# Fused attention and two MLPs on one core: q and k loaded as sixteen consecutive tokens per partition, with some events of a hand-made schedule moved

## The chip, the cores and the metric

The kernel runs on one core of one Trainium2 chip. The metric is the device time of one execution in microseconds (us); lower is better. In the rows, PE is the matrix engine (TensorE), DVE VectorE, ACT ScalarE, POOL GpSimd, and SP the engine whose queue issues the DMA transfers. L12 is line 12 of the kernel before.

## What is computed

Eight batches, eight heads, 576 tokens of 64 numbers each go through attention inside chunks of 64 tokens. The result, laid out as 4608 tokens of 512 numbers, goes through two MLPs, all in float32.

```python
    # attention: B, H, S, D = 8, 8, 576, 64; chunk = 64
    scores = scale * np.matmul(q_c, k_c.transpose(0, 1, 2, 4, 3))
    scores = scores - np.max(scores, axis=-1, keepdims=True)
    attn = np.exp(scores)
    attn = attn / (np.sum(attn, axis=-1, keepdims=True) + 1e-09)
    out = np.matmul(attn, v_c)
    ...
    # first MLP: 4608 x 512, 512 x 2048, 2048 x 512
    h = x @ w_in
    r = np.maximum(h, 0.0)
    g = r * r
    return (g @ w_out).astype(np.float32)
    ...
    # second MLP, same sizes
    h = x @ w_in
    h2 = h * h
    h3 = h2 * h
    P = a[0] + a[1] * h + a[2] * h2 + a[3] * h3
    Q = 1.0 + np.abs(b[0]) * np.abs(h) + np.abs(b[1]) * h2
    g = P / (Q + 1e-6)
    return (g @ w_out).astype(np.float32)
```

## The kernel before

**Float32 on PE.** A float32 product is made of three matmuls on the parts hi and lo of both operands (`mm3`, L463 to L467). So every matrix that PE reads is first split: a copy that rounds to hi (`copy`, L220 on ACT, L222 on DVE or POOL) and a subtraction that leaves lo (`split_lo`, L225).

**Two stages.** From 0 to about 560 us attention and the first MLP run interleaved; after that come planned units in which PE has hardly a pause. The first MLP goes over blocks of 512 tokens and 16 slices f of the hidden width. For the slice with number s, `mm_h(s)` makes 12 matmuls into one of two PSUM banks called h; `act1(s)` makes relu (L587) and its square (L588) on ACT, then hi gh and lo gl; `mm_out1(s)` makes 12 matmuls from gh and gl into four accumulators acc. So one s costs PE 24 matmuls, about 5.5 us. `mm_out1(s)` runs two s behind.

**Attention.** Tokens form 36 tiles of 128, treated in pairs. A pair with start t0 (13.55, 18.55, 22.55, 26.55 up to 58.55 by fours, then 62.3 and 66.3; the unit is one s) has these steps:

- at t0, `mm_pv2` (L730, L733) takes the pair before: 64 small matmuls of attention weights and v, into both h banks. They are emptied at t0 + 0.1, by `x2_hi` on ACT and `x2_lo` on DVE (hi and lo, kept in SBUF), or by `x1_raw`, one bank on ACT and one on DVE (sent to DRAM), and only then can the next `mm_h` write them;
- `mm_s` (L706) at t0 makes the scores of the pair's first tile from q and k, one s later those of the second; softmax follows (L775, L790, L795, L800, L807), and a transposition of its result by DVE (`s_tr`, L814) with copies between partitions on ACT (`s_mv`);
- q and k of a pair come in 8 loads (`load_qk`, four for q into the room qs, four for k into ks, some cut in two at a batch's end). In them 32 partitions hold tokens t*32 + r, so every token is a run of 256 bytes. `tr` (L661) turns blocks of 32x32 on DVE: q and k of the first tile and of the second; `tr_mv` copies on ACT what lies in the wrong partitions, and `tr_part` (L672) turns the rest, on 32 partitions at a time, into the places these copies left. A room can be loaded again once it is read. The very first pair has another layout.

**The first MLP's x** of some tiles is also prepared for the unit stage: DRAM to a buffer room (L433), four sums on POOL (L441), hi on ACT (`xq_hi`, L220, 128x7x128), lo on POOL (`xq_lo`, L225, two instructions), and a store (`xq_store`, L458).

**Order.** `manual_schedule` collects events with `at(t, fn, args)`, adds a number from the table `MOVED` if the event's name stands there, sorts by time and issues in that order. The position in that list is the position on every engine the event uses. `mm_out1(s)` stands at s + 2.5, but for the s just before a pair's t0 (s in `early`) at s + 1.551, which is a moment after t0: so PE has `mm_pv2`, `mm_s`, then this one `mm_out1`. For the pair at 26.55 this is the `mm_out1` of s = 25.

Of the kernel before, what the change touches and what calls it, by code (L numbers as in the profile page):

```python
# [99 lines left out]


@with_exitstack
def attn_moe_moe_kernel(
# [1648 lines left out]
```

## Time and profile before

| | us |
|---|---|
| median of 3 runs | 1651.41 (1650.15 to 1653.93) |
| the profiled execution | 1650.9 |
| its span | 1649.1 |
| PE busy in it | 1592.4 (97%) |
| DVE, ACT, POOL busy | 1053.2, 1097.6, 1070.5 |
| PE busy from 560 us on | 1083.36 of 1089.00 |
| granted PE clock, mean | 0.987 of full speed |

PE is the engine that sets the time; a microsecond leaves the total where PE stands idle or runs at a lower clock, and from 560 us on it has almost none of either. The 1.8 us between the profiled time and its span lie outside of the program's instructions.

### The profile page before, as it was taken

Reading aid. Unit: us, or ns where it says so; the run is one execution under the profiler, and the core shown is the slowest. Engines: PE = TensorE matmul, PEld = TensorE weight load, DVE = VectorE, ACT = ScalarE, POOL = GpSimd, SP = SyncE. Lnnn points to the kernel's source line nnn. Section 1 sums busy time; section 2 is a strip of 40 time slices with the busy share of each in tenths; the row PEclk is TensorE's granted clock in tenths of the full one; section 3 lists DMA queues with packets and bytes.
Section 4 is the critical chain, followed back from the end, with each engine's and each line's share of the span. In section 5 each row is a group of like instructions: output and inputs, shape, how many; then the busy total and the mean of one; then the engine's idle time right before and its main releaser. Section 6 shows DMA issues by size and latency. Waiting matters only on the chain.

```text
span 1649.1 us, 26183 instructions
## 1 busy us (share of the span) xinstructions
PE 1592.4 (97%) x9069; PEld 1308.0 (79%) x9069; DVE 1053.2 (64%) x1498; ACT 1097.6 (67%) x1796; POOL 1070.5 (65%) x1065
## 2 busy tenths in 40 slices
PE   8989999999788999999999999999999999999998
PEld 7867777878566888888878888888888888888887
DVE  6877877777552333233327788878877888788640
ACT  5855556667565556455557787888788878777651
POOL 3645264638662888487847885888588857565554
PEclk9989999999899999999999999999999999999999
DMA  9845788887899899988899999989998997666644
GB/s 248 238 110 147 202 246 252 252 241 224 253 276 370 281 296 301 357 276 284 289 386 326 318 302 370 299 268 300 364 304 269 299 364 256 202 208 203 198 148 146
DMA packets 380356, 440.08 MB, mean 267 GB/s; under 512 B 136896, under 2 KB 260032, under 8 KB 379200
## 3 DMA queue, kind: packets, MB, share of 16 engines
q1 hardware_dynamic: 380224, 438.40, 83.0%
q8 instruction: 73, 1.20, 0.3%
q14 instruction: 59, 0.48, 0.1%
HBM read 318.77 MB, written 119.54 MB: 266 GB/s over the span
## 4 chain that ended last, share of the span: by engine, by line
PE 71%; DMA 8%; ACT 5%; DVE 5%; SPq 4%; POOL 4%; issue 2%; DVEq 0%; ACTq 0%; POOLq 0%
PE acc L465 13%; PE acc L467 13%; PE acc L466 13%; PE h L465 11%; PE h L467 11%; PE h L466 11%; DMA w2q<-st 2%; SPq L638 2%; DMA w2o<-st 1%; ACT at L220 1%; DMA qs<-in_q_dram 1%; SPq L622 1%; DMA ks<-in_k_dram 1%; SPq L836 1%; DVE wc L267 1%
## 5 line engine op out<-in xcount | busy, mean ns | idle before, releaser
L225 POOL TENSOR_TENSOR gl<-spare,gh 128x512 fp32r<-128x512 f32 x200 | 269.1, 1348 | 103.5 <-ACT gh L220 95.0
L1128 POOL TENSOR_TENSOR t<-t,r 128x512 f32<-128x512 f32 x144 | 188.0, 1306 | 150.5 <-ACT t L1120 144.4
L465 PE MATMUL h<-x,w 128*128 128x512 f32 (+1 forms) x648 | 256.2, 395 | 8.4 <-ACT spare L580 6.5
L466 PE MATMUL h<-x,w 128*128 128x512 f32 (+1 forms) x648 | 252.7, 390 | 0.3 <-DVE x L225 0.3
L467 PE MATMUL h<-x,w 128*128 128x512 f32 (+1 forms) x648 | 252.4, 389 | 0.0
L465 PE MATMUL acc<-gh,w 128*128 128x512 f32 x576 | 230.3, 400 | 10.2 <-ACT ev L220 5.2
L466 PE MATMUL acc<-gl,w 128*128 128x512 f32 x576 | 227.5, 395 | 0.0
L467 PE MATMUL acc<-gh,w 128*128 128x512 f32 x576 | 227.5, 395 | 0.0
L466 PE MATMUL acc<-w,gh 128*128 128x512 f32 x575 | 223.8, 389 | 0.0
L467 PE MATMUL acc<-w,gh 128*128 128x512 f32 x575 | 223.8, 389 | 0.0
L465 PE MATMUL acc<-w,gl 128*128 128x512 f32 x575 | 223.8, 389 | 0.0
L465 PE MATMUL h<-w,w 128*128 128x512 f32 x416 | 162.1, 390 | 5.1 <-DVE h L1104 3.7
L467 PE MATMUL h<-w,w 128*128 128x512 f32 x416 | 162.2, 390 | 0.0
L466 PE MATMUL h<-w,w 128*128 128x512 f32 x416 | 162.1, 390 | 0.0
L225 DVE TENSOR_TENSOR w<-w 128x512 fp32r<-128x512 f32 x64 | 68.1, 1068 | 131.2 <-ACT w L220 130.1
L465 PEld LDWEIGHTS h<-x,w 128*128 128x128 f32 x648 | 122.8, 190 | 35.6 <-ACT spare L580 7.3
L467 PEld LDWEIGHTS h<-x,w 128*128 128x128 f32 x648 | 122.9, 190 | 25.4
L466 PEld LDWEIGHTS h<-x,w 128*128 128x128 f32 x648 | 123.0, 190 | 24.9 <-DVE x L225 0.5
L465 PEld LDWEIGHTS acc<-gh,w 128*128 128x128 f32 x576 | 110.0, 191 | 37.6 <-ACT ev L220 6.5
L467 PEld LDWEIGHTS acc<-gh,w 128*128 128x128 f32 x576 | 110.0, 191 | 23.4
L466 PEld LDWEIGHTS acc<-gl,w 128*128 128x128 f32 x576 | 110.2, 191 | 22.4
L467 PEld LDWEIGHTS acc<-w,gh 128*128 128x128 f32 x575 | 108.0, 188 | 22.4
(178 smaller groups left out, 3420.3 us busy)
## 6 DMA issues: line engine op xcount, KB each, us to landing
w<-w2o SPq DMA_DIRECT2D x144, 512.0 KB, 4.8
w<-w2q SPq DMA_DIRECT2D x256, 256.0 KB, 5.4
w<-w1q SPq DMA_DIRECT2D x112, 256.0 KB, 5.6
x2q<-xroom SPq DMA_DIRECT2D x32, 896.0 KB, 6.5
st<-in_moe_w_in_dram SPq DMA_DIRECT2D x32, 512.0 KB, 5.5
st<-in_moe_w_out_dram SPq DMA_DIRECT2D x32, 512.0 KB, 6.1
w2q<-st SPq DMA_DIRECT2D x32, 512.0 KB, 4.6
w<-w1r SPq DMA_DIRECT2D x64, 256.0 KB, 5.6
```

The lines of the kernel that those rows point to most:

```text
L220: nc.scalar.activation(out=o, in_=x, func=ACTF.Copy)
L225: eng.tensor_tensor(out=o, in0=x, in1=hi.bitcast(F32), op=ALU.subtract)
L267: nc.vector.scalar_tensor_tensor(out=c, in0=c, scalar=3, in1=st[:, :, 0], op0=ALU.logical_shift_left, op1=ALU.bitwise_or)
L465: nc.tensor.matmul(out=o, lhsT=al, rhs=bh, start=first and i == 0, stop=False, **kw)
L466: nc.tensor.matmul(out=o, lhsT=ah, rhs=bl, start=False, stop=False, **kw)
L467: nc.tensor.matmul(out=o, lhsT=ah, rhs=bh, start=False, stop=last and i == len(pairs) - 1, **kw)
L622: nc.sync.dma_start(out=x[off:off + n, c], in_=v[bb, h0:h0 + 4, ss:ss + n, :].rearrange("h p d -> p h d"))
L638: nc.sync.dma_start(out=x.rearrange("p (t e) d -> p t (e d)", e=2)[Q:Q + 32, off // 32:(off + n) // 32], in_=src[bb, 2 * i + hp, ss:ss + n ...
L836: nc.sync.dma_start(out=x[:, t], in_={"q": q, "k": k_in, "v": v}[nm][0, 4 * k:4 * k + 4, t0:t0 + 128, :].rearrange("h r d -> r h d"))
L1128: nc.gpsimd.tensor_tensor(out=t, in0=t, in1=T["r", b, f], op=ALU.mult)
```

## The change

**Loads.** For every pair but the first, a partition now takes 16 consecutive tokens in one run of 4 KB. The same bytes go to n/16 partitions instead of 32: the 8 loads of a pair have 8 x 512 packets of 256 B before and 8 x 32 of 4 KB after. Pieces of a load that is cut in two now go to, say, 8 and 24 partitions.

**Transpositions.** For the columns of a turned tile to be in token order again, `blocks()` gives DVE an output in which neighbouring elements of a block of 32 lie 16 elements (64 bytes) apart. What is read keeps its shape.

```diff
         if u:
             b, i = divmod(NAT + 2 * u, TPB)
-            Q = 32 * (2 * (hp % 2) + hp // 2)
             for off, n, bb, ss in runs(b * NB, NB):
-                nc.sync.dma_start(
-                    out=x.rearrange("p (t e) d -> p t (e d)", e=2)[Q:Q + 32, off // 32:(off + n) // 32],
-                    in_=src[bb, 2 * i + hp, ss:ss + n, :].rearrange("(t r) d -> r t d", r=32))
+                Q = 32 * (2 * (hp % 2) + hp // 2) + off // 16
+                nc.sync.dma_start(out=x[Q:Q + n // 16].rearrange("p a d -> p (a d)"),
+                                  in_=src[bb, 2 * i + hp, ss:ss + n, :].rearrange("(r t) d -> r (t d)", t=16))
             return
...
     def blocks(x):
-        return x.rearrange("p a (g r) -> p (a g) r", r=32)
+        return x.rearrange("p a j -> p (a j)").rearrange("p (r t) -> p t r", t=16)
```

On DVE the turned tiles around the pair at 26.55 stand in the same places. Before (q, k are the turned tiles, qs, ks the rooms, u and at the softmax's):

```order
L814 STREAM_TRANSPOSE at_2352<-e_2299 128x8x2x32
L661 STREAM_TRANSPOSE q_2371<-qs_626 128x512
L661 STREAM_TRANSPOSE k_2373<-ks_758 128x512
L661 STREAM_TRANSPOSE q_2378<-qs_626 128x512
L661 STREAM_TRANSPOSE k_2380<-ks_758 128x512
L267 SCALAR_TENSOR_TENSOR wc_2375<-wc_2375,st_2252 128x512
L222 CAST gh_2396<-r_2398 128x512
L225 TENSOR_TENSOR gl_2397<-r_2398,gh_2396 128x512
L672 STREAM_TRANSPOSE q_2378<-qs_626 32x512 x2
L672 STREAM_TRANSPOSE k_2380<-ks_758 32x512 x2
```

The same place on DVE after:

```order
L779 STREAM_TRANSPOSE at_2352<-e_2299 128x8x2x32
L626 STREAM_TRANSPOSE q_2371<-qs_626 128x16x32
L626 STREAM_TRANSPOSE k_2373<-ks_758 128x16x32
L626 STREAM_TRANSPOSE q_2378<-qs_626 128x16x32
L626 STREAM_TRANSPOSE k_2380<-ks_758 128x16x32
L233 SCALAR_TENSOR_TENSOR wc_2375<-wc_2375,st_2252 128x512
L188 CAST gh_2396<-r_2398 128x512
L191 TENSOR_TENSOR gl_2397<-r_2398,gh_2396 128x512
L637 STREAM_TRANSPOSE q_2378<-qs_626 32x16x32 x2
L637 STREAM_TRANSPOSE k_2380<-ks_758 32x16x32 x2
```

The order is the same; the eight transpositions of q and k (four of L661, four of L672, in 14 pairs) have the other output.

**The table.** Old entries keep their numbers but one (a weight's `w_join:(0,7,1)`). New are `mm_out1` of s = 8 to 59 at -0.1 (but 17 at +0.165 and 19 at -0.2), s = 4 at +0.35, and some 25 single events, of which a line:

```diff
 MOVED = {
...
+    'xq_hi:2': -1.0, 'mm_pv2:8,9': 0.05, 'mm_out1:17': 0.165, 'w1q_sum2:6': 0.1, 's_norm:17': -0.2,
...
```

On PE, the -0.1 carries the early `mm_out1` across t0 at 11 pairs (13.55 and 22.55 to 58.55). Before, at 26.55, where w_8_91 holds the slices of two `mm_out1` and h is the next `mm_h`:

```order
L465 MATMUL acc_596<-gh,w_8_91 128x512
L466 MATMUL acc_596<-gl,w_8_91 128x512
L467 MATMUL acc_596<-gh,w_8_91 128x512
L733 MATMUL h<-at,v 64x64 x32
L706 MATMUL a<-k,q 64x64 x16
L465 MATMUL acc_593<-gh,w_8_91 128x512
L466 MATMUL acc_593<-gl,w_8_91 128x512
L467 MATMUL acc_593<-gh,w_8_91 128x512
```

The same place on PE after, from the last three matmuls of the early `mm_out1`:

```order
L431 MATMUL acc_596<-gh,w_8_91 128x512
L432 MATMUL acc_596<-gl,w_8_91 128x512
L433 MATMUL acc_596<-gh,w_8_91 128x512
L698 MATMUL h<-at,v 64x64 x32
L671 MATMUL a<-k,q 64x64 x16
L431 MATMUL h<-x_68,w_10_83 128x512
L432 MATMUL h<-x_69,w_10_83 128x512
L433 MATMUL h<-x_68,w_10_83 128x512
```

The 12 matmuls of the early `mm_out1` now stand ahead of `mm_pv2` and `mm_s`, and the next `mm_h` right behind. At 18.55 it is `mm_s` alone that goes ahead of `mm_pv2`; at 62.3 and 66.3 nothing changes on PE.

On POOL one `xq_lo` goes ahead of four sums of weights (`w1q_sum2:6`, L324). Before, with room_4458 the room of `xq_hi(2)` and `xq_lo(2)`:

```order
L314 TENSOR_TENSOR wc<-w_12_85 128x512
L314 TENSOR_TENSOR wc<-w_13_86 128x512
L324 TENSOR_TENSOR ee<-wc 128x256
L324 TENSOR_TENSOR ee<-ee,wc 128x256
L324 TENSOR_TENSOR wc<-wc 128x2x128
L324 TENSOR_TENSOR wc<-wc,ee 128x2x128
L225 TENSOR_TENSOR room_4458<-room_4458 128x4x128
L225 TENSOR_TENSOR room_4458<-room_4458 128x3x128
L441 TENSOR_TENSOR room_4607<-room_4607 128x128 x4
```

After:

```order
L280 TENSOR_TENSOR wc<-w_12_85 128x512
L280 TENSOR_TENSOR wc<-w_13_86 128x512
L191 TENSOR_TENSOR room_4458<-room_4458 128x4x128
L191 TENSOR_TENSOR room_4458<-room_4458 128x3x128
L290 TENSOR_TENSOR ee<-wc 128x256
L290 TENSOR_TENSOR ee<-ee,wc 128x256
L290 TENSOR_TENSOR wc<-wc 128x2x128
L290 TENSOR_TENSOR wc<-wc,ee 128x2x128
L407 TENSOR_TENSOR room_4605<-room_4605 128x128 x4
```

The two instructions of `xq_lo(2)` moved ahead of four. On ACT `xq_hi(2)` moved too: it stood behind the copies of q and k of the pair at 58.55, right ahead of the relu of s = 58, and stands now ahead of the copies of at that come before all these. On SP a handful of loads swap with a neighbour. The stage after 560 us keeps its order.

## Rows read from the trace of the kernel before

**Rows 1.** The page: busy time by engine, granted clock, DMA packets.

```profile
PE 1592.4 (97%) x9069; PEld 1308.0 (79%) x9069; DVE 1053.2 (64%) x1498; ACT 1097.6 (67%) x1796; POOL 1070.5 (65%) x1065
...
DMA packets 380356, 440.08 MB, mean 267 GB/s; under 512 B 136896, under 2 KB 260032, under 8 KB 379200
```

**Rows 2.** Busy time by stretch; columns as in the first line.

```profile
core 0: us, PE busy (x) PEld busy (x) DVE busy (x) ACT busy (x) POOL busy (x), PEclk, DMA share, GB/s
...
320.00:400.00 80.00, 75.93 (x674) 60.97 (x673) 60.45 (x92) 51.90 (x95) 46.95 (x50) 0.98 0.84 240
...
440.00:480.00 40.00, 27.09 (x214) 21.88 (x215) 21.45 (x34) 23.43 (x41) 25.01 (x32) 0.79 0.87 250
...
560.00:1649.00 1089.00, 1083.36 (x4780) 896.58 (x4778) 669.17 (x908) 756.96 (x1188) 773.01 (x764) 1.00 0.85 282
```

**Rows 3.** PE's waits, 0 to 560 us: us in total, times, longest.

```profile
PE h L733 <- ACT spare L580: 10.4, 4, 8.9
PE h L733 <- ACT r L587: 9.6, 7, 2.5
...
PE acc L465 <- ACT ev L220: 5.2, 3, 2.8
```

**Rows 4.** PE in order of time: start, length, instruction, [idle before it, releaser].

```profile
198.84 0.33 PE L733 MATMUL h<-at,v 64*64 64x64 f32 x2
201.68 1.10 PE L733 MATMUL h<-at,v 64*64 64x64 f32 x59 [2.52 <-ACT r L587]
...
446.33 0.47 PE L733 MATMUL h<-at,v 64*64 64x64 f32 x2 [8.86 <-ACT spare L580]
```

**Rows 5.** ACT in order of time, three stretches.

```profile
118.55 1.09 ACT L220 ACTIVATE x<-h 128x512 fp32r<-128x512 f32 x2 [4.95 <-PE h L730]
...
201.03 0.60 ACT L587 ACTIVATE r<-h 128x512 f32<-128x512 f32 x1
...
445.68 0.60 ACT L580 ACTIVATE spare<-h 128x512 f32<-128x512 f32 x1
```

**Rows 6.** DVE in order of time, three stretches.

```profile
119.20 1.29 DVE L225 TENSOR_TENSOR x<-h,x 128x512 fp32r<-128x512 f32 x2
...
200.12 0.98 DVE L225 TENSOR_TENSOR gl<-r,gh 128x512 fp32r<-128x512 f32 x1
...
429.95 0.65 DVE L267 SCALAR_TENSOR_TENSOR wc<-wc,st 128x512 int32<-128x512 int32 x1
...
441.14 0.71 DVE L661 STREAM_TRANSPOSE q<-qs 128x512 f32<-128x512 f32 x1 [8.60 <-DMA qs<-in_q_dram]
```

**Rows 7.** SP, the issuing queue, in order of time, 412 to 440 us.

```profile
420.45 0.38 SPq L458 DMA_DIRECT2D x1q<-room  x1
...
435.97 1.58 SPq L638 DMA_DIRECT2D qs<-in_q_dram  x1
```

**Rows 8.** SP's waits, 412 to 440 us: us in total, times, longest.

```profile
SPq L458 <- POOL room L225: 3.5, 1, 3.5
```

**Rows 9.** POOL in order of time, 407 to 422 us.

```profile
414.83 0.73 POOL L324 TENSOR_TENSOR ee<-wc 128x256 f32<-128x256 f32 x1
...
418.17 2.25 POOL L225 TENSOR_TENSOR room<-room 128x512 fp32r<-128x512 f32 x2
```

**Rows 10.** Busy time by stretch around the longest pause, columns as in rows 2.

```profile
442.00:452.30 10.30, 5.30 (x101) 4.61 (x102) 7.56 (x11) 5.87 (x10) 6.94 (x10) 0.50 0.79 251
```

**Rows 11.** DVE by line and shape, 80 to 520 us: busy, mean ns | idle before.

```profile
L267 DVE SCALAR_TENSOR_TENSOR wc<-wc,st 128x512 int32<-128x512 int32 x28 | 24.0, 864 | 7.3 <-ACT st L261 6.9
...
L672 DVE STREAM_TRANSPOSE q<-qs 32x512 f32<-32x512 f32 x28 | 19.7, 703 | 2.4 <-ACT q L220 1.6
...
L661 DVE STREAM_TRANSPOSE q<-qs 128x512 f32<-128x512 f32 x28 | 18.9, 674 | 10.0 <-DMA qs<-in_q_dram 10.0
L814 DVE STREAM_TRANSPOSE at<-e 128x512 f32<-128x512 f32 x28 | 18.7, 669 | 0.0
```

**Rows 12.** The page's costliest groups: DVE's dearest 512-column instruction.

```profile
L225 DVE TENSOR_TENSOR w<-w 128x512 fp32r<-128x512 f32 x64 | 68.1, 1068 | 131.2 <-ACT w L220 130.1
```

More of the change, by code (lines that the diff above doesn't have):

```diff
@@ L64 @@
     "xh2": 'V', "xh4": 'V'}
-MOVED = {
[34 rows of a table removed]
+MOVED = {'w_words:(0,3,0)': -14.15, 'w_words:(0,0,1)': -13.45, 'w_words:(0,2,0)': -11.949, 'w_load:0,4,0': -11.348, 'w_join:(0,2,0)': -11.648, 'w_load:0,2,1': -11.348, 'w_join:(0,3,0)': -11.847, 'w_load:0,5,0': -10.747, 'w_join:(0,0,1)': -12.246, 'w_load:0,4,1': -13.245, 'w_load:0,6,0': -0.499, 'w_words:(0,1,1)': -0.527, 'w_split:(0,3,0)': -0.202, 'w_join:(0,1,1)': -0.8, 'first:half110': 11.902, 'w_words:(0,4,0)': -0.401, 'act1:1': 0.401, 'load_tok:4,v,v0': 1.799, 'load_qk:0,qs,1': 0.899, 'load_qk:0,qs,2': 0.301, 'w_words:(0,2,1)': -0.236, 'w_split:(0,1,1)': 0.465, 's_exp:4': 0.015, 'w_load:0,5,1': -0.02, 'act1:2': -0.084, 'w_words:(0,5,0)': 0.517, 'w_join:(0,5,0)': 0.201, 'w_join:(0,2,1)': -0.022, 'w_split:(0,5,0)': 0.079, 'a_ps:5': -2.202, 'tr_second:5': 0.597, 'f_tr:4': 0.597, 'f_copy:4,0,0': -0.152, 'w_load:0,7,1': -0.802, 'load_qk:0,qs,3': 1.2, 'f_copy:4,0,1': -0.15, 'w_words:(0,6,0)': 0.149, 'w_words:(0,7,0)': -0.324, 'tr_copy:5,q': 0.602, 'w_split:(0,3,1)': -0.047, 'f_copy:4,1,1': 0.153, 'w_load:0,6,1': 0.068, 'tr_copy:5,k': 0.821, 'load_tok:5,v,v1': 0.497, 'w_join:(0,6,0)': 0.902, 'mm_s:5,5': -0.199, 'w_words:(0,4,1)': 0.597, 'w_join:(0,7,0)': 0.698, 'w_load:0,9,1': -1.239, 'w_split:(0,6,0)': 0.862, 'w_words:(0,5,1)': 0.299, 'w_split:(0,7,0)': 0.501, 'w_load:0,10,0': 0.448, 'w_join:(0,5,1)': -0.001, 's_exp:5': 0.048, 'w_join:(0,4,1)': 0.699, 'w_words:(0,8,0)': 0.1, 'act1:5': 0.001, 'load_qk:0,ks,3': 0.899, 'w_split:(0,4,1)': 0.399, 'w_words:(0,7,1)': -1.2, 'w_join:(0,7,1)': -1.165, 'w_load:0,11,0': 0.662, 'act1:6': -0.154, 'w_load:0,8,1': 1, 'f_tr:5': 0.599, 'w_words:(0,6,1)': 0.551, 'w_load:0,13,0': -0.299, 'w_join:(0,6,1)': 0.201, 'w_load:0,12,0': 0.205, 'w_split:(0,6,1)': -0.048, 'w_load:0,10,1': -1.647, 'w_split:(0,7,1)': -0.546, 'f_copy:5,1,0': 0.549, 'w_words:(0,10,0)': 0.101, 'w_join:(0,10,0)': 0.196, 'tr:6,ks,k': 1.648, 'f_copy:5,1,1': 1.049, 'act1:8': 0.001, 'load_tok:6,v,v0': 1.459, 'w_words:(0,9,1)': -0.39, 'w_split:(0,10,0)': 0.35, 'mm_s:6,6': 0.001, 'tr:7,ks,k': 1.202, 'w_join:(0,8,1)': 0.335, 'mm_s:7,6': 0.6, 'w_split:(0,8,1)': -0.05, 'x2_lo:1,5': 0.752, 'w_join:(0,9,1)': 0.143, 'act1:9': 0.5, 'w_split:(0,12,0)': -0.199, 'w_words:(0,13,0)': 0.102, 'f_copy:6,0,0': -0.45, 'w_load:0,15,0': 0.051, 'w_join:(0,13,0)': -0.249, 'w_words:(0,10,1)': -0.322, 'w_join:(0,10,1)': -0.401, 's_exp:7': -0.05, 'w_split:(0,9,1)': 0.55, 's_norm:7': -0.073, 'w_load:0,11,1': -0.022, 'f_copy:6,1,0': 0.079, 'f_copy:6,1,1': 0.08, 'act1:10': 0.081, 'w_split:(0,13,0)': 0.3, 'w_load:0,12,1': -0.199, 'w_split:(0,10,1)': 0.101, 'f_copy:7,0,0': -0.551, 'w_load:0,13,1': -0.293, 'w_join:(0,15,0)': -0.047, 'w_split:(0,14,0)': 0.349, 'w_load:0,15,1': -1.142, 'f_copy:7,0,1': 0.301, 'f_copy:7,1,0': 0.443, 'f_copy:7,1,1': 0.444, 'w_join:(0,12,1)': -0.248, 'w_words:(0,13,1)': 0.101, 'w_join:(0,13,1)': -0.149, 'w_split:(0,13,1)': 0.601, 'w_words:(0,14,1)': 0.998, 'w_join:(0,14,1)': 0.751, 'w_join:(0,15,1)': 0.252, 'w_split:(0,14,1)': 0.999, 'w_split:(0,15,1)': 0.898, 's_tr:8': 0.85, 's_mv:8': 0.85, 's_tr:9': 1.06, 's_mv:9': 1.06, 'act1:17': 0.799, 'x1_store:34,35': -0.1, 'mm_pv2:8,9': 0.05, 'mm_h:32': 0.05, 'xq_lo:0': 0.6, 'o_lo:1': -0.1, 'mm_out1:4': 0.35, 'load_qk:1,ks,3': -0.2, 'mm_out1:8': -0.1, 'mm_out1:9': -0.1, 'mm_out1:10': -0.1, 'mm_out1:11': -0.1, 'mm_out1:12': -0.1, 'mm_out1:13': -0.1, 'mm_out1:14': -0.1, 'mm_out1:15': -0.1, 'mm_out1:16': -0.1, 'mm_out1:17': 0.165, 'mm_out1:18': -0.1, 'mm_out1:19': -0.2, 'mm_out1:20': -0.1, 'mm_out1:21': -0.1, 'mm_out1:22': -0.1, 'mm_out1:23': -0.1, 'mm_out1:24': -0.1, 'mm_out1:25': -0.1, 'mm_out1:26': -0.1, 'mm_out1:27': -0.1, 'mm_out1:28': -0.1, 'mm_out1:29': -0.1, 'mm_out1:30': -0.1, 'mm_out1:31': -0.1, 'mm_out1:32': -0.1, 'mm_out1:33': -0.1, 'mm_out1:34': -0.1, 'mm_out1:35': -0.1, 'mm_out1:36': -0.1, 'mm_out1:37': -0.1, 'mm_out1:38': -0.1, 'mm_out1:39': -0.1, 'mm_out1:40': -0.1, 'mm_out1:41': -0.1, 'mm_out1:42': -0.1, 'mm_out1:43': -0.1, 'mm_out1:44': -0.1, 'mm_out1:45': -0.1, 'mm_out1:46': -0.1, 'mm_out1:47': -0.1, 'mm_out1:48': -0.1, 'mm_out1:49': -0.1, 'mm_out1:50': -0.1, 'mm_out1:51': -0.1, 'mm_out1:52': -0.1, 'mm_out1:53': -0.1, 'mm_out1:54': -0.1, 'mm_out1:55': -0.1, 'mm_out1:56': -0.1, 'mm_out1:57': -0.1, 'mm_out1:58': -0.1, 'mm_out1:59': -0.1, 'evac1:0,2': -0.1, 'w1q_store:2,0': 0.2, 'xq_hi:2': -1.0, 's_norm:17': -0.2, 'op_hi:4': -0.35, 'load_v:18': 0.2, 'act1:67': 1.0, 's_exp:35': -0.2, 'w1q_sum2:0': 0.1, 'w1q_sum2:1': 0.1, 'w1q_sum2:2': 0.1, 'w1q_sum2:3': 0.1, 'w1q_sum2:4': 0.05, 'w1q_sum2:5': 0.1, 'w1q_sum2:6': 0.1, 'w1q_sum2:7': 0.1, 'load_qk:14,qs,2': 0.2, 'xp_load:2,0': -1.0, 'o_hi:3': -0.35, 'i_load:6': 1.0}
```

34 rows, old and new, of the table MOVED are left out of this document.

## The prediction

> **What bounds the kernel now.** I read the page first [rows 1]: PE is busy 97% of the span, so what is to be had is PE's idle time, some 57 us, and its time at a low clock. The table by stretches [rows 2] shows where: from 560 us on PE is busy 1083.36 of 1089 us at clock 1.00, and nothing of this change is in there. In 320 to 400 us PE is busy 75.93 of 80; in 440 to 480 only 27.09 of 40, at 0.79 of the clock. So the change is worth what it does to PE's pauses before 560 us. Next PE's waits [rows 3]: the largest are those of `mm_pv2` (L733) for the h banks, which relu on ACT must first read: 9.6 us in 7 waits for L587, the longest 2.5, and 10.4 for L580 in 4, of which one pause of 8.9. Waits for the emptying of acc by ACT come to 5.2. Last I went along the engines in order of time at two of these places.
>
> At 199 us [rows 4] PE has begun `mm_pv2` at 198.84, and idles 2.52 us for the relu of s0 = 26, which ACT makes at 201.03, 0.60 long [rows 5]. Meanwhile PE could do another thing: the early `mm_out1`, whose last input gl DVE ends at 200.12 + 0.98 = 201.10 [rows 6].
>
> At 437 us PE idles 8.86, until 446.33 [rows 4]. It waits for the relu at 445.68 [rows 5]; ACT comes to that only behind the copies of q and k, and these wait for DVE, which had been idle 8.60 us and began q's transposition at 441.14, when qs landed [rows 6]. That load was issued at 435.97 and took 1.58 to issue [rows 7]. SP's queue goes strictly in order, and in it stands, earlier, the store x1q at 420.45, which had waited 3.5 us for POOL [rows 7, 8]. POOL, before the lo that this store needs (418.17), did the four sums L324 from 414.83 on [rows 9]. So one chain runs from four small sums on POOL to the longest pause of the kernel.
>
> **The change part by part.**
>
> *The store at 420 us.* `xq_lo(2)` goes ahead of the four sums: it starts 418.17 - 414.83 = 3.34 us sooner, and `xq_hi(2)`, which it needs, was moved up on ACT as well. The store's wait of 3.5 falls to about 0.2, and everything behind it in the queue can come up to 3.34 us sooner: five loads of v, the next room's load, loads and stores of weights, the loads of q and k. The four sums end 2.25 us later than before (the lo's length [rows 9]); they feed a store of weights for the unit stage, long before these are read, so I put nothing down. The issue of the late qs took 1.58 us where the store took 0.38 [rows 7]; with 32 packets in place of 512 it may cost that much too, 1.2 less. Sum 3.34 + 1.2 = 4.5 us off the pause of 8.86. Ends: 0, if something else in the queue holds it as long, and 8.9, the whole pause.
>
> *The clock behind it.* In 442.00 to 452.30 the granted clock is 0.50, PE is busy 5.30 us there [rows 10]: at full clock these are 2.65. A pause of some 4.4 us in place of 8.86 leaves part of it; I take -2, ends 0 and -2.65.
>
> *The early output block.* At 11 pairs the 12 matmuls now stand before `mm_pv2`. What they cover is the wait for relu (L587), 9.6 us in all [rows 3]. What is new: `mm_h` follows `mm_pv2` and `mm_s` at once, and must wait until the h bank is emptied. There are two kinds of pair. Where x stays in SBUF (13.55, 22.55, 34.55, 38.55, 50.55, 54.55), the first bank is free when ACT's hi (118.55) and the first of DVE's two lo are done, at 119.20 + 1.29/2 = 119.85 [rows 5, 6]; `mm_s` is over some 0.9 us sooner. So 0.9 us becomes visible that twelve matmuls covered. Where x goes to DRAM (26.55, 30.55, 42.55, 46.55, 58.55) one copy frees each bank, and about 0.1 is seen. At 26.55 the early block itself waits for gl until 201.10, 2.26 us after 198.84 in place of 2.52: a gain of 0.2 at most. I went through the 11 pairs and 18.55 in this way: four gain 0.65 to 1.7 (18.55, 30.55, 46.55, 58.55, sum -4.65), five lose 0.35 to 0.95 (13.55, 22.55, 34.55, 50.55, 54.55, sum +4.0), three stay within 0.2 (-0.3). Sum -1. Ends: -9.6, if all of these waits go, and 11 x 0.9 = +10, if none does. I stay near the middle, since gl is made by DVE straight after the relu before it, so that the two things PE can wait for are about equally late.
>
> *The transpositions.* 112 of them (8 in each of 14 pairs) now write at a step of 64 bytes. Before they take 0.674 to 0.703 us, whether 128 partitions or 32 [rows 11]. No row shows DVE writing at a step from element to element. Nearest: L814 writes its blocks of 32 words to scattered places for 0.669; L267 reads every second word of one source, in the mean 0.864, yet 0.65 where nothing disturbs it [rows 6, 11]; the dearest 512-column instruction takes 1.068 [rows 12]. So the price is between 0 and about +0.4 each (1.068 - 0.669); a gain can't be excluded, but the element count is the same. I take 0, since L267 undisturbed shows that a step on the read side alone costs nothing, and carry +0.4 as a rival.
>
> The Trainium skill speaks against this part: "Vector Engine (DVE) Microarchitecture Reference", section 5.2 "Measured stream behaviour on trn2", gives 1.054 ns per column when all is contiguous, 1.71 when the destination hops on every element, and 2.50 when it steps by 24 words, full rate needing pairs of adjacent words. By it a transposition of 512 columns would cost an estimated +0.34 to +0.74 us. L267's 0.65 with a source that has no adjacent pairs [rows 6] doesn't agree with that rule for reads of every second word; for writes no row here decides.
>
> *The loads themselves.* 14 pairs x 8 x 512 = 57,344 packets of 256 B become 3,584 of 4 KB, out of 380,356 [rows 1]. The 16 DMA engines are busy 0.84 to 0.87 of the time in this stage [rows 2], so transfers behind these loads land sooner. But PE seldom waits for one: DVE's 10.0 us of waits for qs are nearly all the 8.60 at 441 [rows 6, 11]. I put -1 for this and the remaining single moves together; ends 0 and -5, about what the waits for acc come to [rows 3].
>
> The sum: 1650.9 (the profiled time) - 4.5 - 2 - 1 - 1 = 1642.4. The median lies 0.5 above the profiled run, so 1643.
>
> **The rivals.**
>
> *Slow transpositions (slower).* With +0.4 each, DVE has 8 x 0.4 = 3.2 us more per pair. In 320 to 400 us it is busy 60.45 of 80 [rows 2], so it has about 6.4 us idle per pair of 26 us and can still do the work; but the four L661 stand right before the gl that the early block now needs, and the four L672 before the next gl and the emptying of h. With a slack of about 0.7 us, 2.5 of the 3.2 reach PE at 13 of 14 pairs: +33, so 1676. It decides from about +0.2 each: 1.6 - 0.7 = 0.9 times 13 is 12 us, more than the gain. For it: nothing in the trace writes so. Against: L267. By the skill's upper figure (section 5.2 again) it would be 5.9 us a pair and a time past 1700.
>
> *The gain is given back (no change).* The pause at 437 shrinks, but PE then arrives that much sooner at the next late thing, a store and POOL's chain at 468 us and the emptying of acc, which are bound by POOL and ACT and not by PE. 440 to 480 us has 12.91 us of pauses [rows 2], and POOL is busy there 25 of 40. If 4.5 + 2 comes back there, -1 remains: about 1650.
>
> *The early block waits for gl, and banks are seen at every pair (slower).* Its end is +10 in place of -1, and half of the store's gain stays: 1643 + 11 + 3 = 1657. Against: the reading at 199 us.
>
> *More gain.* All of L587's 9.6 and the whole pause at 437 go: 1643 - 8.6 - 4.4 = 1630, and with a shorter 468, 1624.
>
> *It doesn't do what it says.* The loads do fall to 4 KB by their shapes; that they land sooner may not follow, since 32 packets over 8 to 32 partitions can use fewer DMA engines. Then the 1.2 of the issue goes, and -8 becomes -7, inside the forecast.
>
> **How the numbers follow.** Forecast 0.45, its own range 1630 to 1648; more gain 0.06; given back 0.15; slow transpositions 0.27 (1657 to 1710, half of it under 1676); late gl 0.07. A measurement of this kernel can tell 0.2%, that is 3.3 us, from no change. Faster: 0.45 + 0.06 = 0.51; same 0.15; slower 0.27 + 0.07 = 0.34. The range for 8 in 10 leaves out the upper half of the slow case (0.13) and the end of the large gain: 1626 to 1676.
>
> **What would show it.** In the profile after: the transpositions' mean (0.67 to 0.70: the forecast; 0.9 or more: the rival); DVE's wait for qs at 440 us down from 8.60 to about 4, PE's pause there from 8.86 to about 4.4 and the stretch at clock 0.50 shorter; SP's wait for POOL before the store gone; PE's waits for L587 under 5 us in all, with new ones of under 1 us for DVE's lo at `mm_h`; and from 560 us on the same 1083 us. The forecast is wrong if the pause at 437 keeps its length, or if PE's waits before 437 grow by more than 5 us.

## The result, and the profile after

| | before | after |
|---|---|---|
| median of 4 runs each, us | 1652.63 (1650.15 to 1653.93) | 1668.92 (1667.54 to 1669.44) |
| ratio | | 1.0099 (95% interval 1.0082 to 1.0117) |
| profiled execution, its span | 1650.9, 1649.1 | 1669.08, 1667.3 |
| mean granted PE clock | 0.987 | 0.984 |
| PE busy in 0 to 600 us | 549.09 | 536.82 |

The change made the kernel 1% slower, about 16 us, where 1643 us were forecast. Single executions of one kernel differ by some us (all of the kernel before lie between 1643.82 and 1659.95 us), so a pause that is longer in one trace than in another need not come from an edit; the ratios go over several executions each. Line numbers of after are 34 or 35 lower: L661 and L672 are L626 and L637, L733 is L698, L706 is L671, L465 is L431, L587 is L553, L580 is L546, L814 is L779, L267 is L233, helpers L220, L222, L225 are L186, L188, L191. In the kernels of the experiments they shift by a few more; the names of the tiles tell which instruction it is.

The page of after, the lines of [rows 1]; the loads are indeed in larger packets, and DVE is busy 34 us more:

```profile
PE 1598.8 (96%) x9069; PEld 1309.7 (79%) x9069; DVE 1087.5 (65%) x1498; ACT 1097.2 (66%) x1796; POOL 1070.0 (64%) x1065
...
DMA packets 325667, 440.05 MB, mean 264 GB/s; under 512 B 78624, under 2 KB 201760, under 8 KB 324512
```

Busy time by stretch, columns as in [rows 2]. Before the unit stage PE has lost time (72.01 of 80 where it had 75.93); the unit stage, 18 us later, is what it was:

```profile
320.00:400.00 80.00, 72.01 (x651) 57.06 (x651) 63.11 (x88) 48.26 (x88) 33.67 (x35) 0.96 0.69 221
578.00:1667.30 1089.30, 1083.96 (x4783) 897.26 (x4781) 667.81 (x908) 758.10 (x1190) 774.31 (x766) 1.00 0.84 283
```

DVE's transpositions, 80 to 540 us (busy, mean ns | idle before), against [rows 11]. Each of q's and k's takes 1.05 us where it took 0.67 to 0.70, whatever the number of partitions; the softmax's, whose form didn't change, take what they took:

```profile
L637 DVE STREAM_TRANSPOSE q<-qs 32x512 f32<-32x512 f32 x28 | 29.6, 1058 | 1.0
...
L626 DVE STREAM_TRANSPOSE q<-qs 128x512 f32<-128x512 f32 x28 | 29.5, 1053 | 3.9 <-DMA qs<-in_q_dram 3.7 <-issue 0.2
...
L779 DVE STREAM_TRANSPOSE at<-e 128x512 f32<-128x512 f32 x28 | 18.7, 669 | 0.0
```

PE's waits after, 0 to 580 us, against [rows 3]: us in total, times, longest. The 9.6 us of waits for relu L587 have no row any more; in their place stand DVE's lo for the banks, gl and gh of the early block, and twice as much for acc:

```profile
PE acc L431 <- ACT ev L186: 10.6, 3, 5.7
PE h L698 <- ACT spare L546: 6.9, 4, 5.3
PE h L431 <- DVE x L191: 6.7, 6, 1.9
...
PE acc L432 <- DVE gl L191: 3.6, 5, 1.2
...
PE acc L431 <- ACT gh L186: 2.2, 2, 2.0
...
PE acc L431 <- DVE gh L188: 1.7, 1, 1.7
```

The pair at 26.55 in order of time, first PE. The pause of 2.52 us in `mm_pv2` [rows 4] is now two pauses ahead of the early block, 1.68 for gh and 0.51 for gl:

```profile
206.56 0.50 PE L431 MATMUL acc<-gh,w 128*128 128x512 f32 x1 [1.68 <-DVE gh L188]
207.58 0.50 PE L432 MATMUL acc<-gl,w 128*128 128x512 f32 x1 [0.51 <-DVE gl L191]
```

And DVE: the four transpositions at 1.05 stand ahead of that gh and gl with only L233 between, as the order had them; four more come behind:

```profile
201.85 1.05 DVE L626 STREAM_TRANSPOSE q<-qs 128x512 f32<-128x512 f32 x1
...
204.53 1.03 DVE L626 STREAM_TRANSPOSE k<-ks 128x512 f32<-128x512 f32 x1
...
206.08 0.43 DVE L188 CAST gh<-r 128x512 fp32r<-128x512 f32 x1
206.54 0.98 DVE L191 TENSOR_TENSOR gl<-r,gh 128x512 fp32r<-128x512 f32 x1
```

The long pause, on PE, against 8.86 us in [rows 4]:

```profile
465.75 0.47 PE L698 MATMUL h<-at,v 64*64 64x64 f32 x2 [5.32 <-ACT spare L546]
```

It is 3.5 us shorter. But PE comes to it at 460.4, where it came at 437.5: 23 us were lost on the way, and 3.5 of them came back here.

The stretches up to the pause and from it to the unit stage hold the same work in both kernels (PE's matmuls differ by one and by two records). The first two lines are before, the other two after:

```profile
80.00:437.50 357.50, 336.43 (x2851) 269.96 (x2849) 271.22 (x422) 214.43 (x388) 186.79 (x184) 0.97 0.74 212
437.50:560.00 122.50, 99.44 (x693) 79.84 (x694) 51.16 (x74) 69.88 (x122) 68.71 (x79) 0.92 0.93 303
...
80.00:460.40 380.40, 341.85 (x2850) 270.84 (x2848) 301.64 (x423) 216.24 (x391) 188.21 (x188) 0.96 0.64 202
460.40:578.00 117.60, 98.77 (x691) 78.99 (x691) 55.43 (x73) 67.15 (x118) 64.74 (x74) 0.93 0.92 304
```

Up to the pause PE is idle 38.55 us where it was 21.07, and busy 5.4 us longer with the same matmuls, at a granted clock of 0.96 in place of 0.97. From there on it needs 4.9 us less.

### The profile page after: what moved, and what is told of

It is laid out like the page before. It is cut to its first block, busy times and chain, and to the rows that moved or that the text cites. A ratio compares the mean times of both kernels' runs of the same rounds, so it can differ in the third digit from the quotient of the medians.

```text
span 1667.3 us, 26169 instructions
## 1 busy us (share of the span) xinstructions
PE 1598.8 (96%) x9069; PEld 1309.7 (79%) x9069; DVE 1087.5 (65%) x1498; ACT 1097.2 (66%) x1796; POOL 1070.0 (64%) x1065
## 4 chain that ended last, share of the span: by engine, by line
PE 77%; DVE 7%; DMA 7%; ACT 4%; POOL 2%; SPq 2%; issue 2%; DVEq 0%; POOLq 0%; ACTq 0%
PE acc L431 14%; PE acc L432 14%; PE acc L433 13%; PE h L431 11%; PE h L432 11%; PE h L433 11%; DMA w2q<-st 1%; DVE k L637 1%; DMA ks<-in_k_dram 1%; SPq L604 1%; DMA x<-x1q 1%; SPq L588 1%; DVE gl L191 1%; PE h L698 1%; DVE wc L233 1%
## 5 line engine op out<-in xcount | busy, mean ns | idle before, releaser
L191 POOL TENSOR_TENSOR gl<-spare,gh 128x512 fp32r<-128x512 f32 x200 | 268.6, 1347 | 107.4 <-ACT gh L186 98.9
L431 PE MATMUL h<-x,w 128*128 128x512 f32 (+1 forms) x648 | 257.2, 397 | 15.3 <-DVE x L191 6.7
L431 PE MATMUL acc<-gh,w 128*128 128x512 f32 x576 | 231.3, 401 | 25.5 <-ACT ev L186 10.6
L431 PE MATMUL acc<-w,gl 128*128 128x512 f32 x575 | 223.8, 389 | 0.0
L431 PE MATMUL h<-w,w 128*128 128x512 f32 x416 | 163.2, 392 | 5.4 <-ACT h L186 4.3
L431 PEld LDWEIGHTS h<-x,w 128*128 128x128 f32 x648 | 122.7, 189 | 44.0 <-DVE x L191 7.5
L191 DVE TENSOR_TENSOR w<-w 128x512 fp32r<-128x512 f32 x64 | 66.5, 1042 | 134.8 <-ACT w L186 133.4
L431 PEld LDWEIGHTS acc<-gh,w 128*128 128x128 f32 x576 | 110.7, 192 | 55.4 <-ACT ev L186 11.9
```

The costliest lines, as they stand in the source:

```text
L191: eng.tensor_tensor(out=o, in0=x, in1=hi.bitcast(F32), op=ALU.subtract)
L431: nc.tensor.matmul(out=o, lhsT=al, rhs=bh, start=first and i == 0, stop=False, **kw)
```

## The experiments

Times are medians. A ratio is to executions of the kernel before on the same chip, with its 95% interval in brackets; where us are made of a ratio, it is times 1652. Two theories to begin with: A, the transpositions are the loss; B, the order of the output blocks is.

**The table alone.**

```diff
 # the loads and blocks() of before
-MOVED = {...}   # of before
+MOVED = {...}   # of the changed kernel
```

> The loads and transpositions of before with the new table of moves. Theory A (DVE's transpositions at a step, 1.05 us in place of 0.68, are the loss): the moves alone give what was forecast, 1643 +- 6, transpositions 0.67 to 0.70. Theory B (the early output block, which now waits for gl and acc and leaves the emptying of the banks uncovered, is the loss): 1660 to 1670, with PE's idle time before 440 us near 37 us as after the change.

Measured: 1655.8, ratio 1.004 (1.0018 to 1.0062). The forecast's gain isn't there even with transpositions of the old length, so A isn't all of it; nor is B, which had 1660 to 1670.

**The layout alone.**

```diff
-MOVED = {...}   # of the changed kernel
+MOVED = {...}   # of before
```

> The new loads and transpositions with the old table. Theory A: 1668 or more (the slow transpositions without the gain of the moves, some 1675). Theory B: 1648 to 1653, the old order hides the longer transpositions.

Measured: 1660.51, ratio 1.0066 (1.0034 to 1.0097). Between both theories: the layout costs by itself, but less than A had said.

**The changed kernel with transpositions that write in a row.**

```diff
     def blocks(x):
-        return x.rearrange("p a j -> p (a j)").rearrange("p (r t) -> p t r", t=16)
+        return x.rearrange("p a (g r) -> p (a g) r", r=32)
```

> The changed kernel with transpositions that write 32 words in a row as before; so the tokens of a pair of tiles come out in another order than q, k and v need (that part of the computation is left out, the number of instructions and bytes is the same). Theory A: transpositions back at 0.67 to 0.70 us and 1640 to 1646. Theory B: within 5 us of the changed kernel's 1669.

Measured: 1653.61, ratio 1.0021 (1.0003 to 1.0038). The result has the tokens in the wrong order; as a measurement it shows that of the 16 us some 13 go with this one line.

**The kernel before with transpositions at a step.** The same line the other way.

> The kernel before, loads of 256 byte runs and old table, with transpositions that write at a step of 64 bytes (token order wrong, number of instructions the same). Theory A: transpositions 1.05 us and 1665 to 1680. Theory B: 1650 to 1655. Against the layout alone it also shows what the 4 KB loads give: a third theory (the long runs themselves are worth much) expects the layout alone to be 5 us or more below this one.

Measured: 1661.44, ratio 1.0078 (1.0052 to 1.0105). Its DVE rows, 80 to 520 us, with loads of 256 byte runs:

```profile
L661 DVE STREAM_TRANSPOSE k<-ks 128x512 f32<-128x512 f32 x28 | 29.6, 1057 | 7.2 <-DMA ks<-in_k_dram 7.2
...
L814 DVE STREAM_TRANSPOSE at<-e 128x512 f32<-128x512 f32 x28 | 18.7, 669 | 0.0
```

So the transpositions are slow by the write at a step, with the old loads too: +0.38 us each, and 0.8% of the time by that alone. The layout alone, with its 4 KB loads, is not 5 us under this, as the third theory had it, but 0.9. PE comes to the long pause here at 446.5 us; up to there:

```profile
80.00:446.50 366.50, 336.68 (x2852) 269.68 (x2851) 298.35 (x422) 214.68 (x389) 188.40 (x187) 0.97 0.73 208
```

Against 80 to 437.5 us of before, 96 transpositions took 34.8 us more in all. DVE is busy 27.1 us more, as others of its instructions took less, and idle 18.1 us less; PE comes 9.0 us later.

**The output blocks alone.** The kernel before with the new entries of `mm_out1` and `mm_pv2`.

```diff
+    'mm_out1:8': -0.1, ..., 'mm_out1:17': 0.165, ..., 'mm_pv2:8,9': 0.05,
```

> The kernel before with only the new entries of the table for the output blocks (mm_out1) and mm_pv2. Theory C (the early block trades relu's wait for three others: gh and gl of its own slice, the acc banks, and 0.96 us for a bank at every pair whose x stays in SBUF): PE's pauses between 80 and 437 us grow by 4 to 8 us against the kernel before, 1655 to 1660. Theory D (the trade is even, as the forecast had it): 1650 to 1653.

Measured: 1661.59, ratio 1.0062 (1.0044 to 1.008). Theory C, and more than it said. PE's waits in this kernel from 80 to 437 us, where relu was the largest before:

```profile
PE acc L431 <- ACT ev L186: 6.8, 3, 3.8
PE h L431 <- DVE x L191: 5.8, 6, 1.0
PE acc L432 <- DVE gl L191: 4.1, 4, 1.2
...
PE acc L431 <- DVE gh L188: 1.3, 1, 1.3
PE h L431 <- ACT xraw L186: 1.2, 5, 0.2
PE h L699 <- ACT r L553: 0.3, 1, 0.3
```

9.3 us of relu are gone, 5.8 + 4.1 + 1.3 + 1.2 = 12.4 are new, and the waits for acc grew by 1.6: 4.7 more in the sum. PE comes to the long pause at 445.5 us, 8.0 later than before, as its matmuls up to there were also busy 3.4 us longer (339.88 against 336.43, with five records more). And in this trace the pause is longer, 11.44 us against 8.86:

```profile
456.96 0.47 PE L699 MATMUL h<-at,v 64*64 64x64 f32 x2 [11.44 <-ACT spare L546]
```

**`xq_hi(2)` and the sums alone.** The kernel before with these entries.

```diff
+    'xq_hi:2': -1.0, 'w1q_sum2:0': 0.1, ..., 'w1q_sum2:7': 0.1,
```

> The kernel before with only the moves of xq_hi(2) and the sums w1q_sum2. Theory E (the store's chain holds as forecast): the pause at 437 us falls from 8.9 to 4 or 5 us and the time by 4 to 6, 1645 to 1648. Theory F (given back at the next late thing, the pause at 468 us): the pause is shorter, the time 1650 to 1653.

Measured: 1649.95, ratio 0.9979 (0.9955 to 1.0003): a gain of some 3 us that the interval just doesn't separate from none. The trace is of the longest of ten executions, 1655.5 us. In it PE's pause at 437 is 3.4 us, under the 4 to 5 of theory E, but another one is longer, at the pair before, 1.00 + 4.23 where it was 2.20:

```profile
418.23 0.33 PE L699 MATMUL h<-at,v 64*64 64x64 f32 x2 [1.00 <-ACT r L553]
422.78 1.45 PE L699 MATMUL h<-at,v 64*64 64x64 f32 x44 [4.23 <-ACT r L553]
```

ACT in the same kernel shows why. The moved copy waits 6.27 us for POOL's sums (which had waited 2.79 us for the room's load), and the copies of at, q and k and the relu that PE waits for stand behind it:

```profile
414.88 0.95 ACT L186 ACTIVATE room<-room 128x896 fp32r<-128x896 f32 x1 [6.27 <-POOL room L407]
```

**The changed kernel without the output blocks' entries.**

```diff
-    'mm_out1:...': ..., 'mm_pv2:8,9': 0.05,   # all of the new ones
```

> The changed kernel without the entries for mm_out1 and mm_pv2: new loads, transpositions at a step, the other moves. Theory C: 6 to 10 us under the changed kernel's 1669, since gl and the emptying of the banks, both behind the longer transpositions on DVE, are covered again: 1657 to 1662. Theory D: 1665 to 1670.

Measured: 1658.92, ratio 1.0037 (1.0015 to 1.0059): theory C, without these entries some 10 us go.

**The same with transpositions that write in a row.**

```diff
-        return x.rearrange("p a j -> p (a j)").rearrange("p (r t) -> p t r", t=16)
+        return x.rearrange("p a (g r) -> p (a g) r", r=32)
```

> The same with transpositions that write 32 words in a row (token order wrong, number of instructions the same): the 4 KB loads and the moves of xq alone. Theory C and E: the fastest of all, 1642 to 1647. Theory F or D: 1650 to 1654.

Measured: 1646.16, ratio 0.9965 (0.9947 to 0.9983). With 4 KB loads, the moves of xq and the other single moves of the table, without the step and the output blocks, the kernel is faster than before (its tokens are in the wrong order).

**The changed kernel once more.**

```diff
 # no edit
```

> The changed kernel once more beside the others, to have all parts on one chip. The parts alone measured +9.3 (transpositions at a step), +9.2 (output blocks), -2.5 (xq) and some -2 (4 KB loads), together +14: if they simply add, 1666; if the longer transpositions make the uncovered waits worse, 1668 to 1672.

Measured: 1667.96, ratio 1.0092 (1.0057 to 1.0126). The parts' ratios multiplied (step 1.0078, blocks 1.0062, xq 0.9979, loads 0.998 from the run below) give 1.0099: they add up, with no sign of an interaction. Each has an interval of some +-0.2%, and the table's other single moves are in none of them; so a few us either way could hide.

**Runs of four words.** Could the layout be had without the step? Here DVE writes 4 words in a row, and PE undoes the order.

```diff
     def blocks(x):
-        return x.rearrange("p a j -> p (a j)").rearrange("p (r t) -> p t r", t=16)
+        return x.rearrange("p a j -> p (a j)").rearrange("p (s t j) -> p t s j", s=8, j=4)
...
+                    y, z = y.rearrange("p (j t) -> p j t", j=4), z.rearrange("p (t j) -> p j t", j=4)
...
-                                         rhs=a_[h][half(c), :, p], start=True, stop=True)
+                                         rhs=a_[h][half(c), :, p].rearrange("k x (t j) -> k j x t", j=4), start=True, stop=True)
```

> 4 KB loads, no entries for mm_out1, and transpositions that write runs of 4 words (16 bytes) with a hop of 64 words: the 64 queries of a chunk then lie side by side in another order, which mm_s (k) and mm_pv2 (weights) undo by reading at a step of 4 words on PE. All of the computation is there. If it is single words at a step that cost, the transpositions are back at 0.67 to 0.70 us and the time is 1644 to 1648, as with 32 words in a row; if any hop costs, 1.05 us and 1657 to 1660; if PE's reads at a step cost, L706's and L733's groups are longer than 0.65 and 1.1 us.

Measured: 1660.3, ratio 1.0047 (1.0029 to 1.0065). DVE's row, 80 to 540 us:

```profile
L629 DVE STREAM_TRANSPOSE q<-qs 128x512 f32<-128x512 f32 x28 | 18.8, 671 | 0.7 <-DMA qs<-in_q_dram 0.7
```

So runs of four words cost DVE nothing. The price went to PE; its groups of scores and outputs over the whole kernel:

```profile
L677 PE MATMUL a<-k,q 64*64 64x64 f32 x1024 | 36.4, 284 | 0.0
L703 PE MATMUL h<-at,v 64*64 64x64 f32 x896 | 33.0, 289 | 13.3 <-ACT r L553 9.2 <-ACT spare L546 4.1
```

In the kernel before the same two groups had 23.3 us (225 ns) and 20.8 (231). The price of PE's step was in none of the expected times.

**The same with the old table and the sums.**

```diff
-MOVED = {...}
+MOVED = {...}   # of before, and w1q_sum2
```

> The same, with the table of before and of the new entries only those of w1q_sum2, so that ACT's copy xq_hi(2) stays behind q and k. Theory G (xq_hi moved up holds ACT and with it the relu before the pair at 58.55 whenever the room's data come late): the pause at 413 us stays at 2 to 3 us and that at 437 at 4, 1642 to 1645. If G is wrong: as the kernel with xq_hi moved, or 3 us above.

Measured: 1661.89, ratio 1.0057 (1.0036 to 1.0079). Not under the one above: no gain from leaving `xq_hi` where it was is seen. The 1642 to 1645 expected left out PE's step, so they decide nothing on G.

**The sums alone.** The kernel before with these entries.

```diff
+    'w1q_sum2:0': 0.1, ..., 'w1q_sum2:4': 0.05, ..., 'w1q_sum2:7': 0.1,
```

> The kernel before with the entries of w1q_sum2 alone. Theory G: pause at 413 us near 2, at 437 near 4 to 5, time 1645 to 1648, below the 1650 with xq_hi moved too. If G is wrong: the same 1650 or the 1652 of before.

Measured: 1652.25, ratio 1.0004 (0.9982 to 1.0026). The trace (1655.5 us) has the pause of 2.3 us at 413 that theory G expects, and 6.0 at 437, where it expects 4 to 5 and before has 8.86. The time is not the 1645 to 1648 of G; the interval, from 3 us less to 4 us more, can't tell whether these 2.9 us are gained.

**Reads at a step in place of PE's.** The keys are put in order when DVE turns the softmax's result, the queries when the banks are emptied.

```diff
-        e = T.pop(("e", t)).rearrange("p b a (x j) -> p (b a) x j", j=32)
+        e = T.pop(("e", t)).rearrange("p b a (w q) -> p (b a) q w", q=4).rearrange("p b (x g) w -> p b x g w", x=2)
...
+            T["x2", ts[-1]] = [x.rearrange("p t b (s j) -> p t b j s", j=4) for x in T["x2", ts[-1]]]
```

> 4 KB loads, the table without the entries for the output blocks, transpositions of q and k that write runs of 4 words; PE reads everything in a row again, and the order inside a chunk is undone where it costs no extra instruction: the keys when DVE turns the softmax's result (L787 reads at a step of 4 words), the queries when the h banks are emptied (ACT and DVE read PSUM at a step of 4 words). All of the computation is there. If reads at a step are free on DVE and ACT: 1644 to 1648, the transpositions 0.67 to 0.71, below the kernel before. If they cost as single-word writes do (0.37 each on DVE, 56 + 14 instructions, and at the banks): 1653 to 1658.

Measured: 1663.29, ratio 1.0065 (1.0048 to 1.0082). DVE, 80 to 540 us: the softmax's transpositions that read SBUF at 4 words' step are as slow as those that wrote at 16, while the emptying of a bank, a read of PSUM at the same step, costs what it did:

```profile
L787 DVE STREAM_TRANSPOSE u<-e 128x512 f32<-128x512 f32 x28 | 30.6, 1094 | 0.6
L787 DVE STREAM_TRANSPOSE at<-e 128x512 f32<-128x512 f32 x28 | 29.6, 1056 | 0.0
...
L188 DVE COPY xraw<-h 128x512 f32<-128x512 f32 x8 | 5.5, 686 | 16.4 <-PE h L701 16.4
```

**The five pairs whose x goes to DRAM.** On the kernel before.

```diff
+    'mm_out1:25': -0.1, 'mm_out1:29': -0.1, 'mm_out1:41': -0.1, 'mm_out1:45': -0.1, 'mm_out1:57': -0.1,
```

> The kernel before with the early output block ahead of mm_pv2 only at the five pairs whose x goes to DRAM (26.55, 30.55, 42.55, 46.55, 58.55). The prediction's sum by pairs gave these -4.2 us together, and the others +3.4: 1647 to 1649. If the early block's own waits (gh, gl, acc) eat that as in the run with all pairs: 1651 to 1656.

Measured: 1668.56, ratio 1.009 (1.0065 to 1.0116). It doesn't answer the question: moved alone, the early block passed the block ahead of it as well (s = 24 stands at 26.5, s = 25 now at 26.451), so PE came 2.7 us sooner to a gh that wasn't ready (a pause of 3.93 us at 194).

**The loads alone.** 4 KB runs, transpositions in a row, old table.

```diff
-        return x.rearrange("p a j -> p (a j)").rearrange("p (r t) -> p t r", t=16)
+        return x.rearrange("p a (g r) -> p (a g) r", r=32)
...
-MOVED = {...}   # of the changed kernel
+MOVED = {...}   # of before
```

> 4 KB loads and transpositions that write 32 words in a row (token order wrong, number of instructions the same) with the old table: the loads alone. If the 4 KB runs are worth something by themselves, 1646 to 1650 with DVE's waits for qs and ks under the 18 us of before and PE's pause at 437 us shorter; if the gain of the kernel with the moves of xq and long runs (-6) needs these moves, 1650 to 1653.

Measured: 1649.01, ratio 0.998 (0.9968 to 0.9992): the loads are worth some 3 us. DVE's wait for qs, 10.0 us in [rows 11], is 5.0 in this kernel (80 to 520 us), and PE's pause at 437 is 4.2 us in its trace, without any move:

```profile
L660 DVE STREAM_TRANSPOSE q<-qs 128x512 f32<-128x512 f32 x28 | 18.9, 674 | 5.0 <-DMA qs<-in_q_dram 4.9
```

**No step in SBUF at all.** As the kernel with reads at a step, but the keys put in order at the subtraction of the maximum, from PSUM.

```diff
+        for a in range(2):
+            nc.vector.tensor_tensor(
+                out=e[:, a].rearrange("p b (j w) -> p b j w", j=4), in0=x[:, a].rearrange("p b (w j) -> p b j w", j=4),
+                in1=m[:, a].to_broadcast([128, HP, D]).rearrange("p b (j w) -> p b j w", j=4), op=ALU.subtract)
```

> As runs4_read, but the softmax's transpositions read 32 words in a row again (they had cost 1.06 to 1.09 us at a step); the keys are put in order where DVE subtracts the maximum, reading the scores from PSUM at a step of 4 words, in two instructions of half the size; queries at the emptying of the banks, where the step on PSUM had cost nothing (0.686 us). All of the computation is there. If PSUM reads at a step are free here too, DVE has only some 0.1 us more per tile: 1645 to 1649, below the kernel before. If they cost 0.37 per tile: 1650 to 1655.

Measured: 1647.3, ratio 0.9972 (0.9955 to 0.999). It has all of the computation and beats both kernels: 5 us under before, some 21 under the change. DVE, 80 to 540 us: twice 0.420 for the subtraction that took 0.69, and every transposition in its old time. The second fence is its busy time from 0 to 600 us, PE's first, 7.3 us more than before's 549.09, in an execution of 1641.2 us:

```profile
L767 DVE TENSOR_TENSOR e<-a,m 128x256 f32<-128x256 f32 x56 | 21.2, 420 | 1.0
...
L640 DVE STREAM_TRANSPOSE q<-qs 32x512 f32<-32x512 f32 x28 | 19.7, 703 | 2.5 <-ACT q L186 1.7
...
L629 DVE STREAM_TRANSPOSE q<-qs 128x512 f32<-128x512 f32 x28 | 18.8, 673 | 0.5 <-DMA qs<-in_q_dram 0.5
```

```profile
0.00:600.00 600.00, 556.36 (x4512) 452.02 (x4513) 403.41 (x636) 370.30 (x658) 340.97 (x344) 0.98 0.79 246
```

Beside the reads at a step this also shows that the place of a slow transposition counts: the softmax's 56 at +0.39 us are 22 us more of DVE and stand for 0.93% of the time, some 15 us (1.0065 against 0.9972); the 112 of q and k, 43 us more of DVE, cost some 13.

**The five DRAM pairs again**, with the block ahead of each early one moved too.

```diff
+    'mm_out1:24': -0.1, 'mm_out1:25': -0.1, 'mm_out1:28': -0.1, 'mm_out1:29': -0.1, ...
```

> The run of five pairs again, with the output block ahead of each early one moved by the same -0.1; without that the early block had passed it too and stood 2.7 us further ahead than in the changed kernel. The walk along the pairs: -4.2 us, 1649. If gh and gl are waited for as in the run of all pairs (1.2 + 1.3 at 26.55, 1.2 at 30.55, 0.7 at 58.55): PE's pauses at these pairs sum to 5 us as in the kernel before, 1652 to 1655.

Measured: 1650.61, ratio 0.9992 (0.9977 to 1.0006). No loss and no clear gain. PE's waits, 80 to 437 us, show an exchange: relu fell from 9.6 to 1.7, but acc grew from 5.2 to 8.3, and gh, gl and xraw are new:

```profile
PE acc L431 <- ACT ev L186: 8.3, 3, 4.9
...
PE acc L431 <- DVE gh L188: 2.6, 2, 1.3
...
PE acc L432 <- DVE gl L191: 1.8, 2, 1.2
PE h L699 <- ACT r L553: 1.7, 3, 0.7
PE h L431 <- ACT xraw L186: 1.2, 5, 0.2
```

All waits there sum to 22.0 us against 20.8 before. PE comes to the long pause at 438.25, 0.8 later than before, and the pause is 11.29 in this trace (of an execution of 1655.17 us).

**The six pairs whose x stays in SBUF.** The same for s = 12, 21, 33, 37, 49, 53 and the s before each.

```diff
+    'mm_out1:11': -0.1, 'mm_out1:12': -0.1, 'mm_out1:20': -0.1, 'mm_out1:21': -0.1, ...
```

> The complement: the early output block ahead of mm_pv2 at the six pairs whose x stays in SBUF (13.55, 22.55, 34.55, 38.55, 50.55, 54.55). The prediction put down +3.9 us for these; the five DRAM pairs alone measured -0.8%o. If the banks' 0.96 us at six pairs is all, 1656 to 1659; if the whole +9 of the output blocks sits here, 1660 to 1663; if below 1655, the two halves cost only together.

Measured: 1663.07, ratio 1.0057 (1.0036 to 1.0078). Nearly the whole cost of the blocks sits here. PE's waits, 80 to 560 us, in a trace of the longest execution (1668.33 us): the banks' 5.8 us, as in the run of all pairs, and relu grew from 9.6 to 14.2, at pairs where nothing was moved:

```profile
PE h L699 <- ACT r L553: 14.2, 7, 3.8
...
PE h L431 <- DVE x L191: 5.8, 6, 1.0
```

The growth of relu need not come from this edit. Two thirds of it, at 26.55 and 30.55 (3.56 where 2.52 was, 3.50 where 1.44 was), stand at the same length in the trace of `xq_hi(2)` and the sums alone, where no output block was moved:

```profile
203.37 1.82 PE L699 MATMUL h<-at,v 64*64 64x64 f32 x59 [3.57 <-ACT r L553]
...
233.17 1.10 PE L699 MATMUL h<-at,v 64*64 64x64 f32 x59 [3.56 <-ACT r L553]
```

## Why the prediction was wrong

**The transpositions: the step that failed first.** The term was put at 0 with +0.4 as a rival; it measured +0.38 each, 0.78% of the time by itself. The row it was put by was the wrong neighbour: L267's 0.65 us is a read at a step of two words. At four words a transposition's read from SBUF costs 0.39 more (reads at a step), its write at sixteen 0.38. The row that differed in the right thing, a write of single words at a step, wasn't in the trace, as the prediction said; then the middle of its bounds was due, and not an end. The rule of the Trainium skill that the prediction weighed and set behind L267 ("Vector Engine (DVE) Microarchitecture Reference", section 5.2 "Measured stream behaviour on trn2": full rate needs runs of at least two adjacent words) forecast this: its estimate was +0.34 to +0.74, and the four-word runs at 0.67 to 0.70 bear out its other half. L267's 0.65 remains against it, for a step of two words.

**What a slow transposition costs: the rival was mis-sized.** It said 2.5 of 3.2 us per pair reach PE, +33. Measured +0.78% alone (0.52 to 1.05), about 13 us, 0.9 us per pair of the 3.0 added. The slack of 0.7 us that it took was too small: with the step alone 34.8 us of longer transpositions made PE 9.0 us late, the rest went into DVE's idle time (18.1) and into other instructions of DVE that took less. That 1669 lies near this rival's 1676 is luck: of its 33 us there were 13, and 10 more came from the output blocks.

**The output blocks: -1 forecast, about +10 measured** (1.0062). This step failed too. The 0.9 us for a bank was right (0.96 in six pairs), and that relu's wait goes, too (9.6 to 0.3). Two things failed in the walk along the pairs. It put down about +4 for the six SBUF pairs, where few waits for relu stood that could be had in return: these alone measure 1.0057, some 9 us. And it took the saved waits of the five DRAM pairs, -4.2 in the sum, as saved time: they are within no change (0.9992), as the early block's own inputs and acc were waited for instead (22.0 us of waits against 20.8). The rival of the late gl and the visible banks had its price right (+10), and a chance of 0.07.

**The store's chain: right in direction.** In after the pause fell from 8.86 to 5.32, with -4.5 forecast. The signs named for it came: SP's wait of 3.5 us for POOL is gone, the late load was issued in 0.74 us in place of 1.58, and DVE's wait for qs there is 3.69 in place of 8.60. One trace each is thin, as the pause varies: 6.1 to 11.4 us over the traces with the old loads and without these moves, 3.4 and 4.7 with the moves (before_xq, moves_only). But the 4 KB loads alone gave 4.2, too. What the prediction left out is `xq_hi(2)` on ACT: it named the move and put nothing down for it. In the trace of these moves alone it held relu by some 4 us, as the room's data came late. Alone they measure 0.9979, some -3.5 us, with an interval that includes no change.

**The clock:** -2 forecast. The same matmuls were busy 5.4 us longer up to the long pause (granted clock 0.96 against 0.97) and 0.7 less behind it (0.93 against 0.92). That the many shorter pauses cost this fits the rows, but no run tests it.

**The loads:** -1 forecast, about -3 measured (0.998). The packets under 512 B fell by 58,272 in the records (57,344 by the count of the loads); most of PE's waits have nothing to do with them, the pause at 437 us has.

**The unit stage:** unchanged, as forecast.

A slip in the sum of one rival: when 4.5 + 2 of the 8.5 come back, -2 remains and not -1; its 1650 stays about right.

What stays open: where the rest of the cost of the six SBUF pairs comes from. Their banks' 5.8 us, less the relu they had, explain about half of the 9 us, and the longer relu of other pairs isn't shown to be an effect of them. And whether the moves of xq gain at all beside the loads: 0.9965 with them against 0.998 without has overlapping intervals.

## What to carry to other kernels

Before a layout is made friendlier to DMA, see which engine then has to step through memory word by word, how often, and what waits behind it: here 112 instructions at +0.38 us outweighed 54,000 saved packets four to one, and runs of four words together with a step taken on the PSUM side kept the gain. Moving work in front of a wait pays only if its own inputs are earlier than that wait and if nothing else was covered by it where it stood.
